# A head pair laid out anew for all engines: bit-moved weights, the fold off TensorE, double score banks and joined exponentials in an attention and feed-forward kernel

## The chip, the cores and the metric

One core of one Trainium2 chip. The metric is device time in microseconds (us), the median of several executions. A profile is of one execution, and its span is some 2 us shorter than the time of that execution (before: 1107.3 of 1109.11 us).

## The reference

```python
# q, k, v: (8, 12, 448, 64); g_q, g_k: (64,); all float32
q_n, k_n = rmsnorm(q, g_q), rmsnorm(k, g_k)
scores = q_n @ k_n^T / sqrt(64)
attn = softmax(scores)                      # over 448 keys
x = (attn @ v) -> (3584, 768)               # tokens by heads x 64
h = x @ w_in                                # 768 -> 1024, weights are doubles in memory
solu = h * softmax(h)
y = layernorm(solu) * g_ln @ w_out          # 1024 -> 768
```

The kernel goes through 48 head pairs (8 batches, 6 pairs each) and 28 feed-forward tiles of 128 tokens. Weights arrive as 64-bit floats and are turned into 32-bit floats on the chip, in 12 pieces of w_in (512 columns) and 16 of w_out (384 columns).

## The kernel before

One instruction stream per engine, laid out by hand in "units" (one piece of TensorE work and what is issued with it); each engine works strictly in its own order. PSUM is the memory that this kernel's products are written to; a slot is one buffer of a rotating pool there. The names in code and profile: qk are queries and keys, qkn the normalised and qkT the transposed ones; part and ss are their sums of squares, from which a first value (the seed) and nx, ny make the inverse roots; s are scores, E their exponentials, es the sum of E over the key parts, o the product with v, sm the row sums, r and xT what the division makes of them; h is x @ w_in, hmax its maximum, u its softmax, pu and uT the transposed u, po the output product. The parts (cuts marked with `# ...`):

```python
ps_h = tile_pool(name="ps_h", bufs=1, space=PSUM)      # h: two banks
ps_t = tile_pool(name="ps_t", bufs=6, space=PSUM)      # six single banks for all else

def convert_w(step, raw):                              # a piece of weights
    def fields():   # VectorE
        tensor_scalar(tmp[:, 1], hi, 0xFFFFF, None, bitwise_and)
        tensor_scalar(e, hi, 20, 0x7FF, logical_shift_right, bitwise_and)
    def scale():    # ScalarE: mantissa to 1.x, exponent rebased
        ...
    def join():     # VectorE: three instructions
        ...
    def product():  # w_in: GpSimd; w_out: VectorE with the gain
        gpsimd.tensor_tensor(dst[:, c, cols], m, e, mult)
    return [fields, scale, join, product]              # a stage in each unit

def fold_sums(n):   # adds the two half sums of a row, on TensorE
    matmul(d["ss"], fold, d["part"])

def scores(n, kc):  # two heads, a bank each, then an exponential each
    for h in range(2):
        s = d["s", h] = ps_t.tile([SP, S], tag="t")
        matmul(s, k_part, q_part)
    for h in range(2):
        scalar.activation(d["E"][:, kc, h], d["s", h], Exp)
    if kc: later(1, lambda: add(n, kc))

def add(n, kc):     # sums over the four key parts
    if kc == 1: gpsimd.tensor_tensor(d["es"], d["E"][:, 0], d["E"][:, 1], add)
    else:       vector.tensor_tensor(d["es"], d["es"], d["E"][:, kc], add)

def ff_in2(t):      # second half of h = x @ w_in, then the softmax steps
    ff_in(t, 1)
    later(1, lambda: ff_max(t))       # VectorE maximum, ScalarE exponential
    later(2, lambda: ff_moments(t))
    later(3, lambda: ff_norm(t))

for n in range(48):  # up to five feed-forward steps (RATE) in each pair
    while at < len(events) and len(due) < RATE and events[at][0] <= n: ...
    # scores 0, scores 1, steps, values(n-1), sums(n-1), steps, scores 2, scores 3, steps
```

Of the kernel before, what the change touches and what calls it, by code (L numbers as in the profile page):

```python
# [366 lines left out]
def fast_path(  # L367
# [9 lines left out]
    within: bass.AP,  # L377
):
# [25 lines left out]
    ps_t = ctx.enter_context(tc.tile_pool(name="ps_t", bufs=6, space=bass.MemoryType.PSUM))  # L404
# [3 lines left out]
    fold = consts.tile([P, 2, 2, 32], FP32, name="fold")  # L408
# [4 lines left out]
    m896 = consts.tile([P, 1], FP32, name="m896")  # L413
    eps = consts.tile([P, 1], FP32, name="eps")

    def setup():

        nc.scalar.add_instruction(
            mybir.InstLoadActFuncSet(
                act_func_set_id=6, name=nc.get_next_instruction_name(), engine=mybir.EngineType.Activation  # L420
            )
        )
        nc.gpsimd.memset(mhalf, -0.5)
        nc.gpsimd.memset(m896, -896.0)
        nc.gpsimd.memset(eps, 1e-6)
        nc.gpsimd.memset(ones, 1.0)
        make_identity(nc, ident)

        nc.gpsimd.memset(fold, 0.0)
        for g in range(4):  # L430
            gs = slice(g * 32, g * 32 + 32)
            for x in range(2):
                nc.gpsimd.tensor_copy(fold[gs, g // 2, x], ident[gs, gs])
        pg = ps_t.tile([P, KF + 2], FP32, tag="t", name="pg")
        nc.tensor.transpose(pg, grow, ident[0 : KF + 2, 0 : KF + 2])
        nc.vector.tensor_copy(gcol, pg)

        nc.vector.tensor_scalar(
            gcol[:, KF : KF + 1], gcol[:, KF : KF + 1], gcol[:, KF + 1 : KF + 2], within, OP.mult, OP.mult
        )  # L440
# [5 lines left out]

    def load_w(step):
        src, _, c, cols = step
        n = cols.stop - cols.start
        raw = work.tile([P, n, 2], U32, tag="raw", name="raw")  # L450
        nc.sync.dma_start(
            raw.rearrange("p n t -> p (n t)"),
            src[c * P : (c + 1) * P, :].bitcast(U32)[:, 2 * cols.start : 2 * cols.stop],
        )
        return raw

    def convert_w(step, raw):

        _, dst, c, cols = step
        n = cols.stop - cols.start  # L460
        lo, hi = raw[:, :, 0], raw[:, :, 1]
        tmp = work.tile([P, 2, n], U32, tag="uT", name="tmp")
        e, m = tmp[:, 0], tmp[:, 1].bitcast(FP32)
        ei = e.bitcast(I32)

        def fields():
            nc.vector.tensor_scalar(tmp[:, 1], hi, 0xFFFFF, None, OP.bitwise_and)  # L467
            nc.vector.tensor_scalar(e, hi, 20, 0x7FF, OP.logical_shift_right, OP.bitwise_and)

        def scale():  # L470
            nc.scalar.activation(m, tmp[:, 1], AF.Copy, scale=2.0 ** -20, bias=1.0)
            nc.scalar.activation(ei, ei, AF.Relu, bias=m896)

        def join():
            nc.vector.scalar_tensor_tensor(m, lo, 2.0 ** -52, m, OP.mult, OP.add)  # L475
            nc.vector.tensor_scalar(ei, ei, 255.0, 2.0 ** 23, OP.min, OP.mult)
            nc.vector.scalar_tensor_tensor(e, hi, 0x80000000, e, OP.bitwise_and, OP.bitwise_or)  # L477

        def product():
            if dst is w_in:  # L480
                nc.gpsimd.tensor_tensor(dst[:, c, cols], m, e.bitcast(FP32), OP.mult)
            else:

                nc.vector.scalar_tensor_tensor(
                    dst[:, c, cols], m, gcol[:, c : c + 1], e.bitcast(FP32), OP.mult, OP.mult
                )

        return [fields, scale, join, product]
# [21 lines left out]
    def load_v(n):  # L510
        b, hp = divmod(n, NP)
        d = st[n]
        d["v"] = loads.tile([SP, 2, NJ, D], FP32, tag="v", name="v", bufs=3)
# [11 lines left out]

    def fold_sums(n):
        d = st[n]
        d["ss"] = ps_t.tile([P, 2 * NB], FP32, tag="t", name="ss")
        nc.tensor.matmul(d["ss"], fold.rearrange("p h x t -> p (h x t)"), d["part"], start=True, stop=True)  # L529

    def rsqrt_seed(n):
# [5 lines left out]
        nc.vector.tensor_scalar(d["x"], d["ss"], -0.5 / D, -0.5e-6, OP.mult, OP.add)  # L537
# [27 lines left out]
    def scores(n, kc):  # L565
        d = st[n]
        if kc == 0:
            d["E"] = work.tile([SP, NJ, 2, S], FP32, tag="E", name="E")
        for h in range(2):
            hh = slice(h * D, (h + 1) * D)  # L570
            s = d["s", h] = ps_t.tile([SP, S], FP32, tag="t", name="s")
            nc.tensor.matmul(  # L572
                s, d["qkT"][hh, 1, kc * SP : (kc + 1) * SP], d["qkT"][hh, 0, :], start=True, stop=True
            )
        for h in range(2):
            nc.scalar.activation(d["E"][:, kc, h], d["s", h], AF.Exp)  # L576
        if kc:
            later(1, lambda: add(n, kc))
# [9 lines left out]
    def values(n):  # L588
# [3 lines left out]
        d["o"] = ps_t.tile([P, S], FP32, tag="t", name="o")  # L592
# [7 lines left out]
    def sums(n):  # L600
        d = st[n]
        d["sm"] = ps_t.tile([P, S], FP32, tag="t", name="sm")
# [4 lines left out]
        later(1, lambda: divide(n))  # L607

    def divide(n):
# [5 lines left out]
        r = work.tile([P, NB, 32], FP32, tag="r", name="r")  # L615
# [53 lines left out]
    def ff_transpose(t):  # L669
        d = mt[t]  # L670
        d["uT"] = work.tile([P, KF, P], FP32, tag="uT", name="uT")
        for half in range(2):
            pt = ps_t.tile([P, 4, P], FP32, tag="t", name="pu")
            for i in range(4):
                c = 4 * half + i
                nc.tensor.transpose(pt[:, i], d["u"][:, c * P : (c + 1) * P], ident)  # L676
            (nc.vector.tensor_copy if half else nc.scalar.copy)(d["uT"][:, 4 * half : 4 * half + 4], pt)  # L677
# [29 lines left out]
    def unit(f):  # L707
# [7 lines left out]
        feed()  # L715
# [6 lines left out]
    W_OUT = 22  # L722
    raws = []
    stages = []
    wdone = 0
    wtarget = 0

    def feed():

        nonlocal wdone  # L730
        for c in list(stages):
            c.pop(0)()
            if len(c) == 1 and len(raws) < len(wq):
                raws.append(load_w(wq[len(raws)]))
            if not c:
                stages.remove(c)
        if wdone < min(wtarget, len(wq)) and len(stages) < 2 and not (stages and len(stages[-1]) > 2):
            stages.append(convert_w(wq[wdone], raws[wdone]))
            wdone += 1
# [22 lines left out]
    def prepare(n):  # L762
        squares(n)
        row_sums(n)

    N = B * NP
    load(0)
    setup()
    load_v(0)
    raws.append(load_w(wq[0]))  # L770
    load(1)
    raws.append(load_w(wq[1]))
    load(2)
    load_v(1)
    with tc.manual_schedule():
        prepare(0)
        wtarget = 1
        unit(lambda: fold_sums(0))
        rsqrt_seed(0)
        rsqrt_step(0)  # L780
        normalise(0)
        prepare(1)
        qk_transpose(0)
        gain(0)
        unit(lambda: fold_sums(1))
        load(3)
        rsqrt_seed(1)
        rsqrt_step(1)
        prepare(2)
        wtarget = 2  # L790
        normalise(1)
        RATE = 5
        at = 0
        for n in range(N):
            due = []
            while at < len(events) and len(due) < RATE and events[at][0] <= n:
# [3 lines left out]
            def ff(k, due=due):  # L800
# [3 lines left out]
            def convert(x):  # L804
                nonlocal wtarget
                if n < W_IN:
                    wtarget = max(wtarget, -(-n_in * (6 * n + x) // (6 * W_IN)))
                else:
                    wtarget = n_in + -(-(len(wq) - n_in) * (6 * (n - W_IN) + x) // (6 * (W_OUT - W_IN)))

            if n + 4 < N:
                load(n + 4)
            if n + 3 < N:
                squares(n + 3)
            convert(1)
            unit(lambda: scores(n, 0))
            if n + 1 < N:
                qk_transpose(n + 1)
                later(1, lambda n=n: gain(n + 1))
            convert(2)  # L820
            unit(lambda: scores(n, 1))
            if n + 2 < N:
                fold_sums(n + 2)
                later(1, lambda n=n: rsqrt_seed(n + 2))
                later(2, lambda n=n: rsqrt_step(n + 2))
                later(3, lambda n=n: normalise(n + 2))
            ff(0)
            convert(3)
            if n:
                unit(lambda: values(n - 1))  # L830
            if n + 3 < N:
                row_sums(n + 3)
            if n and n + 1 < N:
                load_v(n + 1)
            convert(4)
            if n:
                unit(lambda: sums(n - 1))
            ff(1)
            convert(5)
            unit(lambda: scores(n, 2))  # L840
            convert(6)
            unit(lambda: scores(n, 3))
            ff(2)
        unit(lambda: None)
        unit(lambda: values(N - 1))
        unit(lambda: sums(N - 1))
        for _, f in events[at:]:
            unit(f)
        for _ in range(4):
# [4 lines left out]
def kernel(  # L854
# [21 lines left out]
    flag = gains.tile([1, 1], I32, name="flag")  # L876
    nc.scalar.dma_start(grow[0:KF, :], moe_g_ln.rearrange("(c p) -> c p", p=P))
# [8 lines left out]
    nc.vector.tensor_scalar(flag, gmax[0:1], 80.0 / float(D) ** 0.5, None, OP.is_gt)  # L886
    nc.vector.tensor_scalar(within, gmax, 80.0 / float(D) ** 0.5, float(D) ** -0.5, OP.is_le, OP.mult)
    fast_path(tc, q, k, v, moe_w_in, moe_w_out, out, grow, within)
    large = nc.values_load(flag[0:1, 0:1], min_val=0, max_val=1)
    with tc.If(large > 0):  # L890
# [31 lines left out]
```

## Time and profile before

| | before |
|---|---|
| device time, median | 1112.28 us (3 runs), 1111.47 with the run beside the changed kernel |
| span of the profile | 1107.3 us |
| stage A, pairs 0 to 12 | 143.9 us, 11.1 a pair |
| stage B, pairs 13 to 22 | 175.8 us |
| stage C, pair 23 to the first product of the tail | 628.9 us |
| tail | 141.0 us |

The stages are cut at the first score product of pairs 0, 13 and 23, at the first feed-forward product after the last sums, and at the end. The prediction cut C and the tail 3.8 us earlier, so it has 625.1 and 144.8. How to read the profile's lines: a timeline line has start and length in us, engine, line of the kernel, operation, output from input, shapes, count, and in brackets how long the engine sat idle before and what ended that. Busy totals of the kernel before:

```profile
PE 1035.3 (93%) x3617; PEld 475.6 (43%) x3617; DVE 605.4 (55%) x1018; ACT 370.6 (33%) x773; POOL 240.3 (22%) x155
```

PE is TensorE, DVE VectorE, ACT ScalarE, POOL GpSimd.

### The profile page before, as it was taken

How to read it: one execution, taken by the hardware profiler on the slowest of the kernel's cores; microseconds unless marked ns; L12 is line 12 of the kernel's file. 1: busy time of each engine (PE TensorE's matmuls, PEld its weight loads, DVE VectorE, ACT ScalarE, POOL GpSimd, SP SyncE). 2: the span in 40 equal slices, each digit the busy share in tenths (PEclk: the TensorE clock that was granted, in tenths of full speed). 3: DMA queues.
4: the chain of work that ended last, by engine and by line, in shares of the span. 5: the costliest groups of instructions: out<-in, count | busy, mean ns of one | idle time of the engine just before them, and what ended most of it. 6: DMA issues, size and time to landing. Idle time of an engine off the chain costs nothing.

```text
span 1107.3 us, 10659 instructions
## 1 busy us (share of the span) xinstructions
PE 1035.3 (93%) x3617; PEld 475.6 (43%) x3617; DVE 605.4 (55%) x1018; ACT 370.6 (33%) x773; POOL 240.3 (22%) x155
## 2 busy tenths in 40 slices
PE   3988888888789999999999999999999999999997
PEld 1323233333234444444444444444444444455554
DVE  3999996569997444444444444454446644522300
ACT  3656553235564222222222222332224322311110
POOL 2565651123223111111111011121112211100000
PEclk9899999998989999999999999999999999999999
DMA  7454544014543111111111111121111100000010
GB/s 140 89 122 98 124 87 85 23 39 93 112 88 62 40 40 40 39 32 33 32 37 40 40 40 39 40 51 40 40 39 40 34 23 24 14 15 15 15 44 31
DMA packets 230391, 57.49 MB, mean 52 GB/s; under 512 B 223152, under 2 KB 223160, under 8 KB 230328
## 3 DMA queue, kind: packets, MB, share of 16 engines
q1 hardware_dynamic: 225984, 45.64, 20.9%
q10 hardware_dynamic: 4344, 11.08, 2.6%
q8 instruction: 30, 0.49, 0.2%
q14 instruction: 33, 0.27, 0.1%
HBM read 45.68 MB, written 11.01 MB: 51 GB/s over the span
## 4 chain that ended last, share of the span: by engine, by line
PE 75%; DVE 14%; issue 4%; ACT 3%; DMA 1%; SPq 1%; ACTq 0%; DVEq 0%
PE po L686 27%; PE h L635 26%; PE s L572 9%; PE o L595 9%; DVE es L586 2%; PE pu L676 2%; PE sm L604 2%; DVE tmp L467 2%; DVE qkT L559 2%; DVE tmp L475 1%; SPq L505 1%; DVE r L619 1%; DVE tmp L477 1%; DVE r L617 1%; PE ss L529 1%
## 5 line engine op out<-in xcount | busy, mean ns | idle before, releaser
L635 PE MATMUL h<-w_in,xT 128*128 128x512 f32 x672 | 305.0, 604 | 11.7 <-DVE u L653 11.7
L686 PE MATMUL po<-w_out,uT 128*128 128x384 f32 x896 | 298.0, 489 | 2.9 <-ACT uT L677 2.9
L686 PEld LDWEIGHTS po<-w_out,uT 128*128 128x128 f32 x896 | 168.3, 190 | 132.9 <-issue 15.0
L572 PE MATMUL s<-qkT 64*112 64x448 f32 x768 | 204.6, 584 | 16.9 <-ACT E L576 6.7
L576 ACT ACTIVATE E<-s 112x448 f32<-112x448 f32 x384 | 178.0, 550 | 110.0 <-PE s L572 109.9
L635 PEld LDWEIGHTS h<-w_in,xT 128*128 128x128 f32 x672 | 126.2, 193 | 167.5 <-issue 162.8
L584 POOL TENSOR_TENSOR es<-E 112x896 f32<-112x896 f32 x48 | 110.5, 2301 | 325.2 <-ACT E L576 318.7
L595 PE MATMUL o<-E,v 112*64 112x448 f32 x768 | 163.9, 572 | 1.2 <-DVE xT L621 1.2
L572 PEld LDWEIGHTS s<-qkT 64*112 64x112 f32 x768 | 76.6, 177 | 136.9 <-issue 73.6
L677 DVE COPY uT<-pu 128x512 f32<-128x512 f32 x28 | 19.2, 687 | 187.3 <-PE pu L676 187.3
L586 DVE TENSOR_TENSOR es<-es,E 112x896 f32<-112x896 f32 x96 | 115.1, 1199 | 10.9 <-ACT E L576 7.8
L663 POOL TENSOR_TENSOR he<-he,mhalf 128x1 f32<-128x1 f32 x28 | 21.7, 774 | 379.2 <-DVE he L662 379.2
L549 POOL TENSOR_TENSOR qkn<-qk,ny 128x896 f32<-128x896 f32 x48 | 83.0, 1730 | 81.6 <-DVE ny L544 35.0
L648 ACT ACTIVATE u<-h,hmax 128x1024 f32<-128x1024 f32 x28 | 31.2, 1114 | 207.3 <-DVE hmax L645 207.3
L687 ACT COPY y<-po 128x384 f32<-128x384 f32 x56 | 26.8, 479 | 213.5 <-PE po L686 213.5
L595 PEld LDWEIGHTS o<-E,v 112*64 112x64 f32 x768 | 53.2, 143 | 86.5 <-issue 80.5
L645 DVE TENSOR_REDUCE hmax<-h 128x1 f32<-128x1024 f32 x28 | 34.3, 1224 | 84.3 <-PE h L635 84.3
L604 PE MATMUL sm<-es,ones 112*64 112x448 f32 x192 | 44.8, 544 | 16.0 <-DVE es L586 14.1
L617 DVE STREAM_TRANSPOSE r<-sm 128x448 f32<-128x448 f32 x48 | 31.0, 646 | 45.8 <-PE sm L604 45.8
L524 DVE TENSOR_REDUCE part<-sq 128x28 f32<-128x896 f32 x48 | 51.7, 1076 | 5.9 <-ACT sq L519 5.9
L519 ACT ACTIVATE sq<-qk 128x896 f32<-128x896 f32 x48 | 45.8, 955 | 23.1 <-ACT y L687 11.3
L559 DVE STREAM_TRANSPOSE qkT<-qkn 128x896 f32<-128x896 f32 x48 | 52.9, 1102 | 0.0
(54 smaller groups left out, 578.7 us busy)
## 6 DMA issues: line engine op xcount, KB each, us to landing
qk<-in_q_dram SPq DMA_DIRECT2D x192, 56.0 KB, 2.6
qk<-in_k_dram SPq DMA_DIRECT2D x192, 56.0 KB, 2.4
v<-in_v_dram SPq DMA_DIRECT2D x48, 224.0 KB, 3.0
out_dram<-y ACTq DMA_DIRECT2D x28, 384.0 KB, 2.3
raw<-in_moe_w_in_dram SPq DMA_DIRECT2D x12, 512.0 KB, 4.2
raw<-in_moe_w_out_dram SPq DMA_DIRECT2D x16, 384.0 KB, 3.4
grow<-in_g_q_dram ACTq DMA_DIRECT2D x2, 0.2 KB
grow<-in_g_k_dram ACTq DMA_DIRECT2D x2, 0.2 KB
```

The source lines that it names most:

```text
L519: nc.scalar.activation(d["sq"], d["qk"].rearrange("p s b d -> p (s b) d"), AF.Square)
L524: nc.vector.tensor_reduce(d["part"], d["sq"], AX, OP.add)
L549: nc.gpsimd.tensor_tensor(d["qkn"], d["qk"].rearrange("p s b d -> p (s b) d"), d["y"].rearrange("p b -> p b ()").to_broadcast([P, 2 * NB, ...
L559: nc.vector.transpose(d["qkT"].rearrange("p s t -> p (s t)"), d["qkn"].rearrange("p b d -> p (b d)"))
L572: nc.tensor.matmul(s, d["qkT"][hh, 1, kc * SP : (kc + 1) * SP], d["qkT"][hh, 0, :], start=True, stop=True)
L576: nc.scalar.activation(d["E"][:, kc, h], d["s", h], AF.Exp)
L584: nc.gpsimd.tensor_tensor(d["es"], d["E"][:, 0], d["E"][:, 1], OP.add)
L586: nc.vector.tensor_tensor(d["es"], d["es"], d["E"][:, kc], OP.add)
L595: nc.tensor.matmul(d["o"][h * D : (h + 1) * D, :], d["v"][:, h, kc], d["E"][:, kc, h], start=(kc == 0), stop=(kc == NJ - 1),)
L604: nc.tensor.matmul(d["sm"][h * D : (h + 1) * D, :], ones[0:SP, :], d["es"][:, h], start=True, stop=True)
L635: nc.tensor.matmul(d["h"][:, hs], xTs[m][:, c, i * P : (i + 1) * P], w_in[:, c, hs], start=(c == 0), stop=(c == KD - 1))
L686: nc.tensor.matmul(po, d["uT"][:, c], w_out[:, c, hs], start=(c == 0), stop=(c == KF - 1))
```

## The change

Intent: less VectorE work for the weights, no fold on TensorE, fewer and larger instructions, and an order in which each engine has its next work ready. It has seven parts:

1. Weight conversion by moving bits: two ScalarE (three for w_out, which takes the gain) and three VectorE instructions, none on GpSimd.
2. The fold of half sums by four GpSimd copies and a VectorE addition.
3. PSUM: two double slots for scores, transposes and output products; two single ones for o and sm; h as before.
4. One exponential for both heads.
5. One feed-forward step a pair until pair 22, then up to four.
6. A new order of the small work inside a pair.
7. The weights are read again in the tail, to check that their range suits the bit moves.

Smaller edits go with these: one instruction of the seed (0.17 us) moves from VectorE to ScalarE, v and r get fewer buffers, and the first loads are ordered anew.

```diff
-    ps_t = tile_pool(name="ps_t", bufs=6, space=PSUM)
+    ps_t = tile_pool(name="ps_t", bufs=2, space=PSUM)
@@ convert_w
-        def fields(): ...   # 2 VectorE        def scale(): ...    # 2 ScalarE
-        def join(): ...     # 3 VectorE        def product(): ...  # GpSimd or VectorE
+        def low_bits():
+            nc.scalar.activation(low, lo, AF.Relu, scale=-(2.0 ** -29), bias=seven)
+            nc.scalar.activation(tmp[:, 1].bitcast(I32), low, AF.Copy, scale=-1.0, bias=7.0)
+        def high_bits():
+            nc.vector.tensor_scalar(t, hi, 3, 0x3FFFFFFF, OP.logical_shift_left, OP.bitwise_and)
+            nc.vector.scalar_tensor_tensor(t, hi, 0xC0000000, t, OP.bitwise_and, OP.bitwise_or)
         def join():
+            nc.vector.tensor_tensor(o, t, tmp[:, 1], OP.bitwise_or)
@@ the fold
+    def swap_sums(n):
+        for g in range(4):
+            nc.gpsimd.tensor_copy(d["ss"][g * 32 : g * 32 + 32], d["part"][o * 32 : o * 32 + 32])
     def fold_sums(n):
-        nc.tensor.matmul(d["ss"], fold..., d["part"], start=True, stop=True)
+        nc.vector.tensor_tensor(d["ss"], d["ss"], d["part"], OP.add)
@@ scores
+        s = ps_t.tile([SP, 2, 512], FP32, tag="t", name="s")
         for h in range(2):
-            s = d["s", h] = ps_t.tile([SP, S], FP32, tag="t", name="s")
-        for h in range(2):
-            nc.scalar.activation(d["E"][:, kc, h], d["s", h], AF.Exp)
+        nc.scalar.activation(d["E"][:, kc], s[:, :, 0:S], AF.Exp)
@@ pairs (cut: the order inside a pair)
-            while at < len(events) and len(due) < RATE and events[at][0] <= n:
+            while at < len(events) and len(due) < (4 if n > W_OUT else 1) and events[at][0] <= n:
+            unit(lambda: scores(n, 0)); add(n - 1, 3); fold_sums(n + 2)
+            unit(lambda: scores(n, 1)); step(); ff(0)
+            unit(lambda: values(n - 1)); add(n, 1); qk_transpose(n + 1); rsqrt_seed(n + 2)
+            squares(n + 3); gain(n + 1); rsqrt_step(n + 2); normalise(n + 2); row_sums(n + 3); step()
+            unit(lambda: sums(n - 1)); swap_sums(n + 3); step(); begin(n + 1); ff(1)
+            unit(lambda: scores(n, 2)); unit(lambda: scores(n, 3)); add(n, 2); ff(2)
@@ tail
+            check_w(x, again[x])         # a minimum and a maximum a piece, then one small test at the end
```

## The prediction

> **What bounds the kernel now.** I read the busy rows of the page over 40 slices (27.7 us each; digits are tenths) first, because one average over the whole program mixes stages with different limits.
>
> ```profile
> PE   3988888888789999999999999999999999999997
> DVE  3999996569997444444444444454446644522300
> PEclk9899999998989999999999999999999999999999
> ```
>
> VectorE (DVE) is full while TensorE (PE) is not, in slices 2 to 6 and 10 to 12; from slice 14 PE is full and DVE half empty. The table of busy time by windows puts numbers to it (window, length, then busy us and count for PE, weight loads, DVE, ACT, POOL, then the granted clock).
>
> ```profile
> 110.00:165.00 55.00, 46.53 (x188) 16.85 (x185) 53.45 (x86) 30.47 (x66) 33.20 (x15) 1.00 0.51 106
> 220.00:275.00 55.00, 47.79 (x165) 18.48 (x163) 44.31 (x83) 24.21 (x52) 14.42 (x9) 0.91 0.32 66
> 275.00:330.00 55.00, 44.13 (x155) 16.42 (x154) 51.29 (x92) 28.90 (x63) 15.70 (x8) 0.88 0.47 97
> 440.00:550.00 110.00, 110.00 (x387) 53.03 (x387) 48.74 (x81) 33.01 (x68) 15.63 (x11) 1.00 0.15 36
> ```
>
> Then I took the start of each of the 48 head pairs from the timeline (the first of a pair's 16 score records). Four stages come out:
> - **A**, pairs 0 to 12, 17.7 to 161.6 us: 11.11 us a pair, DVE 97% busy. One of 12 w_in pieces is converted in each pair.
> - **B**, pairs 13 to 22, 161.6 to 337.4 (175.8 us): 16 w_out pieces, and nine half-tile input products (h). Pairs 13 and 14 hold all nine and take 46.3 and 34.3 us; pairs 15 to 22 take 11.9 on average.
> - **C**, pairs 23 to 47, 337.4 to about 962.5 (625.1 us): PE without a gap; a pair with one feed-forward tile takes 29.55.
> - **Tail**, 144.8 us: 32 feed-forward steps, PE alone.
>
> The wait list of 165 to 245 us (who waited for whom: total, times, longest) shows why the nine products cost more than their work:
>
> ```profile
> PE h L635 <- DVE u L653: 11.7, 3, 3.9
> ```
>
> Only one h buffer exists, so back-to-back tiles wait for the softmax of the last one. Finally the timeline inside stage A:
>
> ```profile
> 99.14 3.17 DVE L586 TENSOR_TENSOR es<-es,E 112x896 f32<-112x896 f32 x2
> 99.30 2.06 POOL L481 TENSOR_TENSOR w_in<-tmp 128x512 f32<-128x512 f32 x1 [2.09 <-DVE tmp L477]
> ...
> 101.31 2.93 POOL L584 TENSOR_TENSOR es<-E 112x896 f32<-112x896 f32 x1
> ...
> 103.25 1.28 DVE L467 TENSOR_SCALAR tmp<-raw 128x512 uint32<-128x512 uint32 x1
> ...
> 104.46 0.41 DVE L468 TENSOR_SCALAR tmp<-raw 128x512 uint32<-128x512 uint32 x1
> ```
>
> Two additions of es take 3.17 us beside the POOL product; alone they take 1.08 each (timeline at 165.33). L467 takes 1.28 behind POOL's es, its like L468 takes 0.41.
>
> **What the Trainium skill says.** (1) "SBUF — State Buffer", Who interferes with whom: DVE and GpSimd share one port pair under an exclusive lock; a DVE instruction with two SBUF inputs, or in a two-port mode, blocks against GpSimd. The 3.17 and 1.28 us above agree. (2) "VectorE: DVE Perf Modes", The TRN2 errata: ScalarE pays a fixed cost per instruction, 172 cycles from PSUM. The trace agrees: 448 elements take 550 ns and 1024 take 1114, a slope of 0.98 ns, so some 110 ns are fixed. (3) "TensorE: Matmul & The Clock Gate", Part 1: idle PE is throttled to half clock. Granted 0.88 to 0.91 from 220 to 330 us agrees; fewer PE gaps there also bring clock. (4) "PSUM — Partial Sum Buffer", Specifications: 8 banks. Before: h takes two and six single tiles the rest. After: h two, two double tiles (scores, transposes, output products), two single ones (o, sm). The rotating slots fall from six to two.
>
> **The change part by part.**
>
> *Weight conversion.* Before, a w_in piece costs DVE 1.28 + 0.41 + 0.68 + 0.42 + 0.69 = 3.48 us a pair in stage A (timeline), and POOL 1.94. After: a shift-and-mask like L468 (0.41), one combining instruction like L477 (0.69), one OR of two SBUF inputs (0.68, estimated from es: 1.08 us at 896 elements) = 1.78. ACT keeps two (0.63, 0.70). For w_out (384 elements) DVE had 0.74 + 0.35 + 0.55 + 0.35 + 0.80 + 0.60 = 3.39 a piece, 5.4 us a pair; after about 0.4 + 0.65 + 0.55 = 1.6, so 2.6 a pair, and one more ACT copy.
> Stage A: 11.11 - 3.48 + 1.78 = 9.4; less about 0.5 because POOL's 1.94 us no longer block es (1.0 us excess before, half of it kept for the other POOL work), plus 0.4 for blocking that lands elsewhere: **9.3**. The next limits are lower: PE 7.2 (below); ACT 4 x 0.96 + 0.72 + 0.95 + 0.68 + 1.33 = 7.5. DVE stays the bound. I leave pair 1 starting near 28.5 and add 1.5 for three weight pieces loaded ahead of the third q/k pair: pair 13 begins at 28.5 + 1.5 + 12 x 9.3 = **141.6** instead of 161.6.
>
> *Order of stage B.* At most one h step a pair until pair 22, so nine steps spread over pairs 13 to 21. PE: 7.2 + 5.42 = 12.6. DVE: attention 7.5 + conversion 2.6 + half a tile's softmax (1.22 + 1.22 + 1.37 + 0.21 + 0.47 + 0.85 = 5.3, so 2.7) = 12.8. Neither hides all of the other: **12.9** for nine pairs, 8.0 for pair 22, 124.1 in all instead of 175.8. Of the 51.7, 11.7 are the h waits, the rest overlap of DVE-bound pairs with PE-bound h work, and clock. Pair 23 begins at **265.7**.
>
> *Fold off PE.* Pairs 41 and 46 have no feed-forward: 7.53 us with the ss product, 7.19 without (no sums are due at pair 46). So ss costs 0.34 a pair; 23 pairs in C give 7.8. Its replacement, four 32-partition POOL copies (0.2 each, as L433's) and a DVE addition of 28 elements (0.17), lies beside PE work.
>
> *Exponentials of two heads at once.* 384 at 0.55 become 192 at about 0.55 + 448 x 0.00098 = 0.99: 20 us of ACT saved in total, none on a path where ACT binds; worth nothing directly.
>
> *Two double slots.* New cost in C: after two score steps a third user of the rotation (a transpose or an output product) needs the first step's slot. Its exponential ends about 0.2 + 0.98 us after it, the second step takes 0.80 (two steps 1.76 at 515.13): 0.35 us stall. Three of five feed-forward steps use the rotation, and two such places occur per pair: 0.42 a pair, 25 pairs, 10. C becomes 625.1 - 7.8 + 10 = **627**. Steps per pair fall from at most 5 to 4, but I counted the lists: 99 steps lie in C and 32 are left, before and after, so this moves no work to the tail.
>
> *Check of the weights.* The tail reads the weights again (12.6 MB) and does 56 reductions, about 0.6 us each (1.22 at 1024), 34 us of DVE. There DVE is idle (17.5 of 60 us from 990 on), and 28 loads in 130 us ask 97 GB/s, below the 141 of the first window. The transposes of the last check may add a little: tail **146**.
>
> Span: 265.7 + 627 + 146 = 1038.7. The median exceeds the profiled span by 5.0; I add a little less since I chose most terms cautiously: **1041 us**, 6.4% less.
>
> **The rivals.** *The two slots bind PE in C.* For it: six slots become two, and ACT serves them in order, so any ACT wait for a maximum on DVE reaches PE. Against: ACT is 30% busy in C, and long h products and the o products, which have slots of their own, lie between. If each pair lost 1.5 us more, about 1078. *POOL becomes the hidden bound of A and B through the port lock.* For it: POOL is 60% busy in stage A and four copies are added. Against: 1.94 us of product go. If nothing of the blocking is relieved, A is 10.2, B 14: plus 21, about 1062. *DVE is relieved so far that PE binds.* A at 8.2 and B at 12.5: minus 17, and without slot stalls minus 10 more, 1014. *The reloaded weights disturb the tail.* DVE in order behind a late load delays a softmax; the tail has four tiles of lead work, so at worst some 10 us.
>
> **Range and chances.** The slot and lock rivals make the upper side, 1070; the full relief the lower, 1012. To be within 2% (above 1090) both bad rivals would have to come together. Faster 0.93, same 0.05, slower 0.02.
>
> **What would show it.** Pair starts: A near 9.3 with DVE over 93% busy; B near 12.9 without the wait of h for u; C near 25 us a pair of four steps with PE over 97% busy, its gaps named as waits on ACT's E; no ss rows; L467's successor near 0.41; exponentials near 0.98. Wrong would be: PE under 95% in C, DVE idle in A (then a chain of waits, not throughput, sets the pair), or a tail above 152 with DVE waiting for raw loads.

## The result

The changed kernel takes 1118.57 us (1117.52 to 1118.92, 4 runs) beside 1111.47 us (1110.53 to 1113.05, 4 runs): ratio 1.0061, 95% interval 1.0043 to 1.0078, so the same at 2% and in truth a little slower. A ratio here is the mean time of one kernel's runs over that of the other's of the same rounds, so not quite the ratio of the medians. The forecast was 1041.

By stage, in us:

| | pair 0 starts | A | B | C | tail | span |
|---|---|---|---|---|---|---|
| before | 17.7 | 143.9 | 175.8 | 628.9 | 141.0 | 1107.3 |
| after | 15.5 | 148.1 | 151.6 | 660.2 | 141.0 | 1116.4 |
| change | -2.2 | +4.2 | -24.2 | +31.3 | 0.0 | +9.1 |
| forecast of the change | 0, with A | -20.0 | -51.7 | +1.9 | +1.2 | -68.6 |

B gave half of what was promised, A nothing, and C took back more than B gave. In A the steady pairs 4 to 11 take 11.1 us before and after; the 4.2 us come from its ends, 3.8 of them from pair 12, the last. The busy rows over 40 slices, the windows and the busy totals of the changed kernel:

```profile
PE   2868769878899989999999999999999999999997
DVE  4999997987874355434455453545554344455521
PEclk8898989999999999999999999999999999999999
```

```profile
110.00:165.00 55.00, 37.34 (x160) 12.39 (x162) 51.90 (x76) 33.75 (x56) 23.53 (x29) 0.91 0.48 102
220.00:275.00 55.00, 45.51 (x153) 16.17 (x151) 45.47 (x72) 29.14 (x50) 19.00 (x25) 0.94 0.34 74
275.00:330.00 55.00, 48.67 (x188) 17.97 (x188) 45.41 (x71) 28.49 (x49) 20.72 (x25) 0.97 0.32 61
440.00:550.00 110.00, 105.29 (x361) 48.83 (x362) 53.45 (x84) 31.49 (x54) 21.76 (x31) 1.00 0.21 44
```

```profile
PE 1002.6 (90%) x3523; PEld 445.3 (40%) x3523; DVE 651.1 (58%) x1013; ACT 383.9 (34%) x645; POOL 258.9 (23%) x326
```

In stage A VectorE is as full as before (51.90 of 55 us, against 53.45), though the conversion of a w_in piece lost two of its five VectorE instructions. In C TensorE has gaps: 105.29 of 110 us instead of 110.00. TensorE's busy total fell by 33 us and nothing came of it. VectorE's rose by 46 us: 34 of these are the check in the tail, which cost no time (141.0 us both ways).

**What fills VectorE in A.** The timeline of the changed kernel in pair 8:

```profile
106.68 3.97 DVE L607 TENSOR_TENSOR es<-es,E 112x896 f32<-112x896 f32 x2
107.55 2.16 POOL L605 TENSOR_TENSOR es<-E 112x896 f32<-112x896 f32 x1 [2.17 <-ACT E L599]
...
110.58 0.17 DVE L553 TENSOR_TENSOR ss<-ss,part 128x28 f32<-128x28 f32 x1
...
113.43 1.70 POOL L573 TENSOR_TENSOR qkn<-qk,ny 128x896 f32<-128x896 f32 x1 [3.73 <-DVE ny L568]
...
114.26 1.41 DVE L471 TENSOR_TENSOR w_in<-tmp 128x512 uint32<-128x512 uint32 x1
```

Two additions that take 1.08 us alone take 3.97: the second one ends 0.9 us after POOL's addition does, and it lists 2.79 us of "busy" time. The OR of the weights takes 1.41, and ends 0.54 us after POOL's qkn; in e8 below, where 11 of 12 lie clear of POOL's work, it takes 0.68. So the order lays a POOL instruction that reads SBUF (the on-chip memory that holds E and qk) beside the two-input VectorE instructions of every pair. Summed over pairs 4 to 11, by how much do VectorE instructions exceed the shortest time of the same operation and shape? Before, 1.8 us a pair: 0.90 in the additions of es, 0.87 in the first step of the conversion. After, 2.5: 0.86 in the additions, 0.73 in the OR, 0.47 in the fold's addition, 0.45 in the second step of the conversion. The blocked share did not fall; it moved and grew.

**What opens the gaps of C.** The wait list of TensorE from 315 to 975 us, and one gap in the timeline:

```profile
PE po L705 <- ACT E L599: 19.9, 20, 2.2
PE s L596 <- DVE uT L696: 6.0, 11, 1.4
PE pu L694 <- ACT E L599: 2.6, 10, 0.3
```

```profile
594.43 1.76 PE L596 MATMUL s<-qkT 64*112 64x448 f32 x8
594.54 1.23 DVE L665 TENSOR_REDUCE hmax<-h 128x1 f32<-128x1024 f32 x1 [3.07 <-PE h L655]
595.80 1.11 ACT L668 ACTIVATE u<-h,hmax 128x1024 f32<-128x1024 f32 x1 [7.49 <-DVE hmax L665]
...
596.90 1.71 ACT L599 ACTIVATE E<-s 112x896 f32<-112x896 f32 x2
...
597.86 2.53 PE L705 MATMUL po<-w_out,uT 128*128 128x384 f32 x7 [1.67 <-ACT E L599]
```

Two score steps (594.43) fill both double slots. ACT has stood idle 7.49 us because its next instruction is the tile's exponential, which waits for a maximum on VectorE; only then come the scores' exponentials, and the output product waits for the slot. From the starts of the records: the step from a score product to po takes 0.47 us in the kernel before; after, ten of twenty take 0.80 and ten 2.20 to 2.76, in all 21.2 us too much. The steps to pu add 3.2. Against e9 below, which has the same order and no gap in C, those between scores add 8.0 and those within po 1.7 (one stretch near 400 us, with a granted clock of 0.57): together 34.1 of the 34.4 us by which C is longer than in e9.

### The profile page after: what moved, and what is told of

It is laid out like the page before. It is cut to its first block, busy times and chain, and to the rows that moved or that the text cites. A ratio compares the mean times of both kernels' runs of the same rounds, so it can differ in the third digit from the quotient of the medians.

```text
span 1116.4 us, 10449 instructions
## 1 busy us (share of the span) xinstructions
PE 1002.6 (90%) x3523; PEld 445.3 (40%) x3523; DVE 651.1 (58%) x1013; ACT 383.9 (34%) x645; POOL 258.9 (23%) x326
## 4 chain that ended last, share of the span: by engine, by line
PE 69%; DVE 19%; ACT 7%; issue 2%; POOL 1%; DMA 0%; SPq 0%; ACTq 0%; DVEq 0%; POOLq 0%
PE po L705 27%; PE h L655 24%; PE o L616 9%; PE s L596 6%; DVE es L607 4%; ACT E L599 3%; PE pu L694 2%; PE sm L625 2%; DVE qkT L583 2%; DVE part L540 2%; DVE tmp L467 2%; DVE hmax L665 2%; DVE w_in L471 1%; ACT u L668 1%; DVE tmp L466 1%
## 5 line engine op out<-in xcount | busy, mean ns | idle before, releaser
L705 PE MATMUL po<-w_out,uT 128*128 128x384 f32 x896 | 301.1, 492 | 22.0 <-ACT E L599 19.9
L596 PE MATMUL s<-qkT 64*112 64x448 f32 x768 | 188.5, 608 | 63.2 <-ACT E L599 32.6
L705 PEld LDWEIGHTS po<-w_out,uT 128*128 128x128 f32 x896 | 168.3, 191 | 156.9 <-ACT E L599 34.6
L599 ACT ACTIVATE E<-s 112x896 f32<-112x896 f32 x192 | 166.9, 912 | 96.9 <-PE s L596 96.9
L616 PE MATMUL o<-E,v 112*64 112x448 f32 x768 | 160.1, 560 | 0.0
L605 POOL TENSOR_TENSOR es<-E 112x896 f32<-112x896 f32 x48 | 106.0, 2207 | 180.5 <-ACT E L599 162.1
L596 PEld LDWEIGHTS s<-qkT 64*112 64x112 f32 x768 | 62.4, 182 | 173.7 <-ACT E L599 74.4
L668 ACT ACTIVATE u<-h,hmax 128x1024 f32<-128x1024 f32 x28 | 31.2, 1113 | 156.9 <-DVE hmax L665 156.9
L625 PE MATMUL sm<-es,ones 112*64 112x448 f32 x192 | 45.3, 550 | 15.5 <-DVE es L607 15.5
L566 DVE TENSOR_TENSOR nx<-nx,ny 128x28 f32<-128x28 f32 x48 | 28.7, 597 | 50.3 <-ACT ny L562 50.3
L549 POOL COPY ss<-part 32x28 f32<-32x28 f32 x192 | 49.2, 256 | 20.7 <-DVE part L540 11.8
```

The source lines that it names most:

```text
L596: nc.tensor.matmul(s[:, h, 0:S], d["qkT"][hh, 1, kc * SP : (kc + 1) * SP], d["qkT"][hh, 0, :], start=True, stop=True)
L599: nc.scalar.activation(d["E"][:, kc], s[:, :, 0:S], AF.Exp)
L605: nc.gpsimd.tensor_tensor(d["es"], d["E"][:, 0], d["E"][:, 1], OP.add)
L616: nc.tensor.matmul(d["o"][h * D : (h + 1) * D, :], d["v"][:, h, kc], d["E"][:, kc, h], start=(kc == 0), stop=(kc == NJ - 1),)
L625: nc.tensor.matmul(d["sm"][h * D : (h + 1) * D, :], ones[0:SP, :], d["es"][:, h], start=True, stop=True)
L705: nc.tensor.matmul(po, d["uT"][:, c], w_out[:, c, hs], start=(c == 0), stop=(c == KF - 1))
```

## The experiments

Each run's stages, in us:

| run | A | B | C | tail | device time | ratio to before |
|---|---|---|---|---|---|---|
| e1_six_banks | 147.8 | 154.7 | 636.3 | 140.7 | 1094.43 | 0.9844 |
| e2_split_exp | 148.4 | 151.4 | 662.0 | 141.1 | 1120.65 | 1.0086 |
| e3_es_write_only | 128.3 | 145.0 | 661.1 | 141.0 | 1092.89 | 0.9836 |
| e4_bits_alone | 159.1 | 177.5 | 629.3 | 139.8 | 1124.72 | 1.0121 |
| e5_softmax_later | 148.2 | 142.7 | 643.6 | 156.9 | 1110.29 | 0.9996 |
| e6_spread_alone | 144.1 | 149.1 | 628.7 | 140.8 | 1084.53 | 0.9767 |
| e7_six_es_dve | 137.6 | 146.8 | 626.3 | 140.6 | 1072.35 | 0.9657 |
| e8_bits_spread_es_dve | 141.1 | 145.4 | 629.3 | 139.8 | 1077.16 | 0.9703 |
| e9_six_esdve_later | 138.0 | 138.6 | 625.8 | 140.4 | 1060.86 | 0.9550 |
| e10_double_esdve_later | 141.0 | 139.1 | 643.6 | 141.1 | 1081.63 | 0.9733 |
| e11_e9_fold_pe | 136.6 | 145.7 | 637.5 | 140.6 | 1079.45 | 0.9706 |
| e12_e9_five | 138.3 | 140.7 | 624.7 | 140.4 | 1062.40 | 0.9557 |

All give correct results but e3, which is wrong on purpose. My theory after the result: C is lost to the two slots, A to POOL's reads. The rivals: the new order itself in C; a ring of in-order waits in A.

**e1_six_banks: the PSUM layout of before in the changed kernel.**

```diff
-    ps_t = tile_pool(name="ps_t", bufs=2)          # double slots, o and sm apart
+    ps_t = tile_pool(name="ps_t", bufs=6)          # single slots for all
-        nc.scalar.activation(d["E"][:, kc], s[:, :, 0:S], AF.Exp)
+        for h in range(2): nc.scalar.activation(d["E"][:, kc, h], d["s", h], AF.Exp)
+        # the transposes of a tile in two halves of one bank each
```

> The changed kernel with the PSUM layout of before put back: six single-bank slots, one exponential per head, the transposes of a feed-forward tile in two halves; order, conversion, fold and check stay as changed. Stages by first score product: A (pairs 0 to 12) 148.1 us, B (13 to 22) 151.6, C (23 to the first product of the tail) 660.2 and tail 141.0 in the changed kernel; 143.9, 175.8, 628.9 and 141.0 in the kernel before. Slot theory: the 32 us that PE loses in C behind scores (20 gaps from scores to po of 21 us above normal, 10 to pu of 3, 11 between scores of 7) are waits for a slot, so C falls to about 628; B falls by some 10, A stays near 146; in all about 1075 to 1082 us. Rival (the new order itself, shorter bursts of feed-forward work between scores): C stays above 650 and the time above 1105.

C fell by 23.9 us to 636.3, and TensorE's waits on ACT there are gone. All that is left in its wait list for C:

```profile
PE s L596 <- DVE r L638: 4.0, 4, 1.0
PE po L707 <- DVE xT L642: 0.3, 1, 0.3
```

A stayed at 147.8. The slots explain most of C's loss and none of A. B did not fall by 10 as expected but rose by 3. The run changes the layout as a whole (six banks, o and sm in the same rotation, transposes in halves); only the exponentials are tested apart, next.

**e2_split_exp: double slots, but one exponential per head.**

```diff
-        nc.scalar.activation(d["E"][:, kc], s[:, :, 0:S], AF.Exp)
+        for h in range(2): nc.scalar.activation(d["E"][:, kc, h], s[:, h, 0:S], AF.Exp)
```

> The changed kernel with its two double slots, but one exponential per head again (384 in place of 192). If the joined exponential matters by itself (slot held longer because both heads must end, or ACT relieved), C or A moves by more than 5 us. My theory: the slot is held by the tile, not by the instruction; two pipelined exponentials took 0.46 us each before and the joined one 0.87 per pair of heads, so ACT gains 11 us over the program where it is not the bound: all stages within 3 us of the changed kernel, the time within 0.5% of 1118.

All stages within 1.8 us of the changed kernel. The joined exponential is worth almost nothing, and is not the cause of the loss. The page rows of before and after show why (busy us in total, then the mean of one in ns):

```profile
L576 ACT ACTIVATE E<-s 112x448 f32<-112x448 f32 x384 | 178.0, 550 | 110.0 <-PE s L572 109.9
```

```profile
L599 ACT ACTIVATE E<-s 112x896 f32<-112x896 f32 x192 | 166.9, 912 | 96.9 <-PE s L596 96.9
```

Back to back, the single ones overlap: 178.0 / 384 is 0.46 us each, not 0.55. Two cost 0.93, a joined one 166.9 / 192, or 0.87.

**e3_es_write_only: POOL about as busy, but without reading E (wrong results).**

```diff
-            nc.gpsimd.tensor_tensor(d["es"], d["E"][:, 0], d["E"][:, 1], OP.add)
+            nc.gpsimd.memset(d["es"], 1.0)
+            nc.gpsimd.memset(d["es"], 2.0)
```

> Wrong results on purpose: POOL no longer adds the first two score tiles into es but fills es twice with a constant, so it is about as busy (some 2 us a pair) and VectorE still waits for it, but POOL no longer reads SBUF there. Port-lock theory: the two VectorE additions, 3.97 us together in stage A, go back to 2.2 and the pair period in A from 11.1 to about 9.3 (A near 125 us), B shorter by 10 or more, C unchanged. Rival (a ring of in-order waits through ACT, VectorE and TensorE sets the pair, and VectorE is only long because it waits anyway): the period in A stays above 10.6.

The pair period in A fell to 9.39 us, at the 9.3 of the theory, and C did not move. The timeline (VectorE's additions still need POOL's result):

```profile
103.80 0.84 POOL L605 MEMSET es<- 112x896 f32 x1
...
104.70 0.84 POOL L606 MEMSET es<- 112x896 f32 x1
...
105.04 2.28 DVE L608 TENSOR_TENSOR es<-es,E 112x896 f32<-112x896 f32 x2
```

All 96 VectorE additions now take 1.07 to 1.09 us, and the fold additions 0.17 to 0.19 instead of up to 2.07. The two fills take 1.7 us against 2.2 for the addition, so POOL is also a little shorter; the 1.8 us of blocking that vanish from one pair are more than that. The fills also do not wait for E, so they start at another time. That does not explain it away: 27 of the additions lie beside a fill for 0.27 to 0.87 us and none is stretched, so it is POOL's reading that stretches them, not its being busy. (The shift-and-mask of the conversion is stretched by a fill too: 1.05 to 1.07 us instead of 0.35 to 0.43, in all six places where one lies beside it.) The ring is not what holds A at 11.1.

**e4_bits_alone: the bit moves in the kernel before.** The diff is the conversion part of the change alone.

> The kernel before with the bit-moved weight conversion alone, everything else as before (order, fold on TensorE, six slots). The prediction's step said 3.48 us of VectorE a piece fall to 1.78 and POOL loses a product of 1.94, so A goes from 11.1 to 9.3 us a pair. If that step was right and the new order spoilt it: A near 121 us in place of 143.9, B near 160, C and tail unchanged, the time about 1072. If the saving of VectorE time is lost to waits whatever the order: A above 138, the time above 1095.

My second figure, and worse: the saving was not only lost, A became slower, 12.88 us a pair, while VectorE was busy 42.66 of 55 us. I read this as a ring in the old order that the bit moves close:

```profile
104.52 2.45 POOL L578 TENSOR_TENSOR es<-E 112x896 f32<-112x896 f32 x1 [0.43 <-ACT E L570]
104.96 4.16 DVE L580 TENSOR_TENSOR es<-es,E 112x896 f32<-112x896 f32 x2
...
109.04 1.10 DVE L553 STREAM_TRANSPOSE qkT<-qkn 128x896 f32<-128x896 f32 x1
...
110.18 0.67 ACT L557 ACTIVATE qkT<-qkT,gcol 128x448 f32<-128x448 f32 x1 [5.73 <-DVE qkT L553]
110.75 0.74 ACT L466 ACTIVATE tmp<-raw,seven 128x512 f32<-128x512 uint32 x1
...
112.36 0.19 DVE L531 TENSOR_SCALAR nx<-ss 128x28 f32<-128x28 f32 x1 [2.22 <-ACT ny L530]
```

POOL's es holds VectorE's additions (4.16 us), these hold the transpose, ACT sits idle 5.73 us for it, then does the new low-bit work ahead of the seed, and VectorE sits idle 2.22 us for the seed. Only POOL's part in this is tested, by e8.

**e5_softmax_later: double slots, the tile's softmax two units later.**

```diff
-        later(1, lambda: ff_max(t)); later(2, lambda: ff_moments(t)); later(3, lambda: ff_norm(t))
+        later(3, lambda: ff_max(t)); later(4, lambda: ff_moments(t)); later(5, lambda: ff_norm(t))
```

> The changed kernel with one number shifted: the softmax steps of a feed-forward tile (maximum, moments, normalisation) are issued two units later, so that the next two score exponentials stand ahead of the tile's exponential in the ACT queue. The six-bank run took 24 us from C; of the 20 gaps from scores to output products in C, half are 0.80 us and half 2.2 to 2.8. Theory: the long ones are ACT waiting for the maximum on VectorE ahead of the score exponential, with both slots full; they fall to 0.80, C from 660 to about 645, A unchanged, the time about 1103. Rival (two slots cost the same however ACT is ordered): C stays above 657.

C fell to 643.6. Times in us of the twenty steps from scores to po in C, from the records' starts:

```
after             10 x 0.80,  9 x 2.20 to 2.21,  1 x 2.76
e5_softmax_later   1 x 0.47, 19 x 0.80
e1_six_banks      19 x 0.46 to 0.47,  1 x 0.81
```

So the long waits are the tile's exponential ahead of the scores' in ACT's queue. B gained 9 us that I had not named. The tail lost 16 (156.9): there nothing fills the two units, and the transposes come late.

**e6_spread_alone: the kernel before with at most one step a pair before pair 23.**

```diff
-            while at < len(events) and len(due) < RATE and events[at][0] <= n:
+            while at < len(events) and len(due) < (RATE if n > W_OUT else 1) and events[at][0] <= n:
```

> The kernel before with one thing changed: before pair 23 at most one feed-forward step a pair instead of five. The prediction's step said that the burst in pairs 13 and 14 costs 11.7 us of waits for the single h buffer, and that spreading also overlaps VectorE-bound pairs with TensorE-bound products. If so, B falls from 175.8 to about 145 (conversion still 3.4 us a piece), A, C and tail stay, the time about 1081. If only the buffer waits go and nothing overlaps, B is about 164 and the time 1100.

B 149.1, the time 2.3% lower with one line. The step on the burst was right in kind; it yields 26.7 us, somewhat more than the whole change got from B.

**e7_six_es_dve: e1 with the first es addition on VectorE.**

```diff
-            nc.gpsimd.tensor_tensor(d["es"], d["E"][:, 0], d["E"][:, 1], OP.add)
+            nc.vector.tensor_tensor(d["es"], d["E"][:, 0], d["E"][:, 1], OP.add)
```

> The changed kernel with the six single slots of the first experiment and the first addition of es moved from POOL to VectorE, correct results. Port-lock theory: VectorE gets 1.08 us more a pair but no longer waits for POOL's reads of E, which cost 1.8 us a pair in A and more in B; A from 147.8 to about 140 (10.4 us a pair), B from 154.7 to about 148, C at 636; the time about 1080. If the VectorE work counts and the lock does not, A goes up by 14 to about 161.

A 137.6 (10.4 in most pairs), although VectorE has more to do; the time 1072.35. C gave another 10 us. The traces show where: in e1 the scores waited four times for VectorE's r (4.0 us, the list above), and in e7 TensorE's wait list for C is empty; the steps between scores are 8.0 us shorter and those within po 1.7.

**e8_bits_spread_es_dve: the kernel before with three parts.** The diffs of e4 and e6 and the one of e7.

> The kernel before with bit-moved weights, at most one feed-forward step a pair before pair 23, and the first es addition on VectorE; its six slots, its fold on TensorE and its order stay. The bit moves alone made A slower (12.9 us a pair, VectorE 78% busy), in a ring in which POOL's es waits behind POOL's qkn and blocks the two VectorE additions (4.16 us). Theory: without POOL in that ring the saved VectorE time shows: A about 9.5 us a pair (124 us), B about 140, C 629, tail 141; the time about 1055. If the ring goes through ACT and VectorE alone: A above 150 and the time above 1085.

A 141.1: better than the 159.1 of e4, so POOL was part of that ring, but far from 124. VectorE is busy 9.4 us of 10.94 a pair, so a chain of waits still holds. Which one was not tested: the profile's own chain of work from 62 to 150 us has 31% in TensorE's product with v and 2.5% in ScalarE's seed, and does not name ACT's low-bit work among its largest parts. The forecast of 1055 was missed by 22 us.

**e9_six_esdve_later: all three findings.** The diffs of e1 and e7, and e5's for all tiles but the last four.

> All three findings together on the changed kernel: six single slots, the first es addition on VectorE, and the softmax of a tile issued two units later for all tiles but the last four (the tail grew by 16 us when they were delayed too). Stages of the run with the first two alone: A 137.6, B 146.8, C 626.3, tail 140.6. The later softmax took 9 us from B and cannot take more than a few from C, where only 2 us a cycle are left: A 138, B 138, C 625, tail 141, the time about 1064. If delaying the softmax in C starves the transposes, C grows above 632.

1060.86 us, ratio 0.9550: better than both kernels. Its windows for A, B and C:

```profile
60.00:150.00 90.00, 75.60 (x306) 25.38 (x304) 87.31 (x139) 59.73 (x129) 22.78 (x40) 0.93 0.50 108
154.00:292.00 138.00, 129.19 (x468) 49.37 (x467) 123.67 (x212) 85.13 (x183) 34.61 (x51) 0.98 0.38 86
292.00:918.00 626.00, 626.00 (x2191) 289.97 (x2188) 307.91 (x517) 194.27 (x419) 68.44 (x135) 1.00 0.18 40
```

TensorE has no gap in C. In A VectorE is still full (87.31 of 90 us), now with work: only the OR is stretched (1.47 for 0.68 us); VectorE's other instructions run at the shortest time of their shape, to 0.03 us a pair.

**e10_double_esdve_later: e9 with the double slots and joined exponentials.**

> The same as the previous run, but with the two double slots and the joined exponentials of the changed kernel. Theory: the long waits behind the tile's exponential are gone, what is left of the two slots is 0.33 us at 20 gaps to po, 10 to pu and some between scores, about 12 us in C: C near 638, A near 138, B near 138, the time about 1076. If the double slots cost nothing once the other two causes are gone: C below 629.

C 643.6 against 625.8: once the order is mended, the double slots still cost 17.8 us, more than the 12 that I gave them. The steps show 6.3 us before po and 3.3 before pu, as forecast, and 8.0 between scores, where the wait list has VectorE's copy of the transposes (PE s <- DVE uT: 6.0 us, 11 times), which frees their slot. A was 141.0, not 138.

**e11_e9_fold_pe: e9 with the fold back on TensorE.**

```diff
-        nc.vector.tensor_tensor(d["ss"], d["ss"], d["part"], OP.add)
+        nc.tensor.matmul(d["ss"], fold..., d["part"])      # and no POOL copies
```

> The combined kernel with the fold of the sums of squares back on TensorE, in place of four POOL copies and a VectorE addition a pair. The prediction gave 0.34 us a pair of C to the fold off TensorE; the gaps of the trace say 0.24 where feed-forward work follows. So C grows by 6 us. POOL loses 1.0 us of copies that read SBUF a pair and VectorE an addition: A and B shrink by 0 to 6 us together. The time within 0.6% of the combined kernel. If the swap was the hidden cost in A and B, A falls below 128.

18.6 us slower than e9 (1.75%), where 0.6% was the most that I gave it. C grew by 11.7 us, 0.5 a pair (24.79 instead of 24.26 for a pair of four steps): here the fold stands between two score steps and breaks their run. B grew by 7. Taking the fold off TensorE was a gain in this order, and no hidden cost of A, which changed by 1.4.

**e12_e9_five: e9 with five steps a pair in C.**

```diff
-            len(due) < (4 if n > W_OUT else 1)
+            len(due) < (5 if n > W_OUT else 1)
```

> The combined kernel with at most five feed-forward steps a pair in C, as in the kernel before, in place of four. Changes between scores and feed-forward products cost TensorE some 0.1 us each in the gaps; with 20 instead of 25 mixed pairs C should fall by about 5 us to 620 and the rest stay: the time 4 to 5 us lower. If the number of changes of kind costs nothing, C stays within 2 us.

C 624.7, the time 1062.40: no gain. My idea that frequent changes of kind eat the fold's gain falls. Pairs of five steps take 29.33 us against 29.55 in the kernel before, and pairs without steps 7.25 against 7.53, so without the fold a pair of the old kind is 0.22 to 0.28 us shorter, not 0.34.

## Why the prediction was wrong

- **Stage A** is the first step that failed: "less about 0.5 because POOL's 1.94 us no longer block es (1.0 us excess before, half of it kept for the other POOL work), plus 0.4 for blocking that lands elsewhere: **9.3**". It left 0.9 us of blocking a pair (the kept half of es and the 0.4); 2.5 were measured. The new order lays POOL's es beside VectorE's additions and POOL's qkn beside the OR. Of the 1.70 us that the conversion was to save, 0.87 was blocking, which moved instead of going. Without POOL's reads of E, 1.8 of these go and the pair takes 9.39 (e3). The rival of the port lock was named, with A at 10.2 and +21 us in all; A came out 24.2 above the forecast, of which e3 gives 19.8 to POOL's reads.
- The method behind it failed as well: I took busy time on the fullest engine, subtracted the work removed, and called the rest the new period. e4 did just this part in the old order and grew by 1.8 us a pair. Busy time on VectorE held waiting for POOL, and where the pair is a ring of in-order waits, where an instruction stands in its queue can count more than work taken from VectorE (ACT is busy 6.8 us a pair in e4, 6.6 before).
- **Stage C**: "0.42 a pair, 25 pairs, 10" measured 32.4 us in the steps (34.1 less the 1.7 within po) and 23.9 when the six slots came back. The term itself was right: 30 stalls of 0.33 us are 9.8. Two terms were missing. Half of the steps to po are 2.2: the tile's exponential is issued ahead of the next scores', which costs another 14.6 (16.6 in e5). And scores themselves wait for the slot of the transposes, 8.0. I had named the first ("any ACT wait for a maximum on DVE reaches PE") and dismissed it because ACT is 30% busy. An engine that is idle because its next instruction waits is not free. The wait is on the short stretch of two score steps, where the long products that I counted on do not stand between.
- **Stage B**: "Neither hides all of the other: **12.9**" measured 16.0 on average over the same nine pairs (pair 22: 7.7 for 8.0). e6 shows that the spread is real (26.7 us). Of what is missing, POOL's reads make 6.6 us (e3) and the late score exponentials 8.9 (e5). With all three causes removed B is 138.6, still 14.5 us above the forecast, with TensorE busy 129 of 138 us in the window. Its wait list there names 8.7 us (VectorE's r 4.0 and xT 1.9, ScalarE's E 2.8); what makes the rest longer than my sum of 12.6 a pair is not settled.
- **Fold**: "23 pairs in C give 7.8" was too much; 0.22 to 0.28 a pair give some 5 or 6. Right in kind.
- **Joined exponentials**: "worth nothing directly" was right (e2), though 11 us of ACT were saved and not 20: I took 0.55 us for a single one, where four in a row take 0.46 each, and a slope between two different instructions (scores and a tile), which gave 0.99 for the joined one. Measured were 0.91: from 550 ns at 448 and 912 at 896 elements, 0.81 ns an element and 0.19 us fixed in a record, not 0.98 and 0.11.
- **Check in the tail**: right; 141.0 us both ways, reductions of 0.54 to 0.68 us.
- **Range**: both bad rivals came true together. POOL's reads cost 26.4 us (e3) for the 21 that I gave the lock, and C came out 29.4 above the forecast for the 37 of the slots. Most of the other 21.9 us of the miss lie in B, where neither rival had put them. The range did not follow from them: its upper end, 1070, lies below the 1078 of the slot rival alone, and both together would be 1099. I had given all outcomes short of a 2% gain 7% together.
- **Signs**: the three signs of being wrong did not show: PE in C 95.7% (105.29 of 110 us), DVE in A 94% (51.90 of 55), the tail 141.0. "DVE over 93% busy" came true though the pair took 11.1 us, because blocked time counts as busy; a sign that shows in both cases tests nothing.

The sum, from the experiments: without POOL's reads the changed kernel has 26.4 us less in A and B, with six slots 23.9 less in C; 1116.4 minus both is 1066.1, and e7, which does both in a correct way, has a span of 1067.1. That the two agree to 1 us is partly luck: in e7 A and B are 11.1 us longer than in e3, as VectorE takes over the addition, and C is 10.0 shorter than in e1.

## What to carry to other kernels

Before subtracting removed work from a full engine, look whether its instructions run at their shortest time; if they do not, what fills it is a wait under another name, and it may move instead of go. Count the slots between a producer and the consumer's next two uses, and look at what is queued ahead of the instruction that frees a slot: an idle in-order engine can still hold it for as long as its next instruction waits. Try the parts of a large change one by one; here one line (spreading the feed-forward steps) was worth 2.3% where the whole was worth nothing.

## What the Trainium skill lacked or had wrong

- "Trainium Kernel Development and Optimization", Best Practices, calls occupancy fine for engines other than TensorE. Here VectorE's occupancy in stage A was 97% before and 97% from 55 to 110 us after (53.45 of 55 us both times) and contained 1.8 and 2.5 us a pair of waiting for POOL; with POOL's reads of E gone a pair took 9.39 us instead of 11.1 (e3). An addition blocked this way showed 2.79 us of busy time against 1.08 free.
- "VectorE: DVE Perf Modes", The TRN2 errata, gives a ScalarE instruction from PSUM a fixed 172 cycles and one for each element: for 448 elements at its 1.2 GHz 517 ns (an estimate from its table). The records show 550 ns on average, but four in a row took 1.83 us, 0.46 each. The section lacks that part of the fixed cost is hidden between such instructions in a row; joining two saved only 0.06 us.
- No page works out that a buffer stays taken for as long as the head of an idle in-order engine waits, so that an order is only as good as the queue ahead of the instruction that frees it: here ten gaps of 2.2 us and more came from a ScalarE that was 30% busy, and putting its waiting instruction two units later took 16.6 us off C (e5).
